# The scaling of a row of summed squares, moved from VectorE into ScalarE's copy of the row

## The chip, the cores and the metric

The kernel runs on one core of a Trainium2 chip. The metric is the device time of one execution in microseconds; the profile is of one execution of the same program.

## What is computed

Three parts follow each other: attention with keys and values pooled by eight (8 batches, 8 heads, 576 positions), a feed-forward block without a nonlinearity, and a second one with a root-mean-square norm ahead of it and a SwiGLU in it. Between the parts the data is a matrix of 4608 tokens by 512 features. The change lies in the norm:

```
a = x @ w1; b = x @ w2; h = a * b @ w3; y = h @ w_out          # first block
rms = sqrt(mean(y * y, axis=-1) + 1e-06); xn = y / rms * rms_g  # norm
g = xn @ w_gate; val = xn @ w_val; out = g * sigmoid(g) * val @ w_out2
```

## The kernel before

Tokens are cut into 9 blocks of 512 (`TB`), held with the features on the partitions: a block of `y` is four tiles of 128 x 512. Every matrix product is done as three products of split operands (`mm3`, lines 104 to 106: high by high, high by low, low by high), so each operand exists as a rounded high part, which ScalarE casts (line 100), and a remainder, which VectorE subtracts (line 101). The two matrices `w3` and `w_out` of the first block are multiplied into one beforehand (`wph`, `wpl`).

The attention and the products with `w1` and `w2` run first, and the products `h` go to DRAM (`hdram`). Then, from about 640 us of the span, the loop of lines 1350 to 1372 takes the nine blocks in the order `OB` (8, 4, 5, 6, 7, 0, 1, 2, 3; `turn` is a block's place in it). For each of eight pieces of a block, `h_load` (line 1311) brings two pieces of `h` into one of three `raw` tiles, `h_split` (lines 100 and 101, tile `hb`) splits them into one of four tiles, and `second` adds 12 matmuls to the block's four PSUM banks. The banks come from two pools of four by the parity of the turn (`ybank`: `ps` or `y`).

After a block, `y_end` squares the four banks on ScalarE (line 679, into `x0b`), copies them out (lines 687 and 689), stores them (line 691, `ydram`) and adds the squares on VectorE (line 693). The rest is a list of steps that the next block's loop takes: `sq_split` splits the sums (ScalarE line 699, VectorE line 701, tile `f`), and four places later `rms` lets TensorE sum them over the partitions with two matmuls by a column of ones into one row of a bank (lines 707 and 708), ScalarE copies the row out of PSUM (line 710), SP stores its 2 KB in DRAM (line 711), POOL loads them back as 128 x 4 (line 713, `ss`), VectorE multiplies by 1/512 and adds 1e-6 (line 714), POOL raises to the power of -0.5 (line 717) and stores the result (line 718, `rdram`). The bank of the row is one of the four that the block after the next block's start needs, so that block's fourth tile waits for the row copy of line 710.

Whoever needs the norm loads `rdram` on all partitions: for block 0, which has turn 5, `xn_steps` does it two turns later (line 1032) and then scales `xr` (line 1042) and splits it (lines 1045 and 1046, `xnh`, `xnl`).

Beside this loop a list of steps (`side`) prepares the weights of the second block: 64-bit inputs are turned into float32 (`Conv`: ScalarE lines 144 and 147, VectorE lines 159, 168 and 171), summed (lines 782 and 933), split (tiles `wst` and `ost`, lines 100 and 101) and stored by POOL (line 798, tensor `wd`; line 943, tensor `od`). The tiles `ost` are used again once their store has landed. SP loads the first weights of the next stage into a ring (`wr`, line 982) as soon as its pieces, used for raw inputs until then, are free.

A scheduler sets the order of the instructions on each engine from these lists and from its own estimates; each engine, and each DMA queue of SP and POOL, then runs in that order.

Of the kernel before, what the change touches and what calls it, by code (L numbers as in the profile page):

```python
# [13 lines left out]
AF = mybir.ActivationFunctionType  # L14
ALU = mybir.AluOpType
# [6 lines left out]
def kernel(  # L22
# [17 lines left out]
    nc = tc.nc  # L40
    B, H, S, D = q.shape
    P = 128
    NT, DM = out.shape
# [25 lines left out]
    def psum():  # L69
        return ps_p.tile([P, 512], F32, tag="ps", name="ps")  # L70
# [8 lines left out]
    def ftile(dt=F32):  # L79
        return f_p.tile([P, 512], dt, tag="f", name="f")  # L80

    def hxtile(nm):
        return hx_p.tile([P, 512], F32R, tag=nm, name=nm)
# [576 lines left out]
    def ybank(i):  # L660
        if turn.get(i, 0) % 2:
            return psum()
        return py_p.tile([P, 512], F32, tag="y", name="y")
# [3 lines left out]
    def bpiece(k):  # L667
        if not x0b:
            for nm in ("xh", "xl"):
                t = x0_p.tile([P, KD, TB], F32R, tag=nm, name="x0b")  # L670
                x0b.extend(t[:, u] for u in range(KD))
        return x0b[k]

    def y_end(i):
        ys = yacc.pop(i)
        sq = []
        for kk in range(KD):
            sq.append(bpiece(kk).bitcast(F32))
            nc.scalar.activation(sq[kk], ys[kk], AF.Square)
            if i == 0:  # L680
                if kk == 0:
                    xr[i, 0] = rtile("xr", F32).rearrange("p (k t) -> p k t", k=KD)
                yc = xr[i, 0][:, kk, :]
            else:
                yc = hxtile("hh" if kk % 2 else "hl").bitcast(F32)
            if kk % 2:
                nc.scalar.copy(yc, ys[kk])
            else:
                nc.vector.tensor_copy(yc, ys[kk])
            if i:  # L690
                nc.sync.dma_start(out=ydram[i, kk], in_=yc)
            if kk:
                nc.vector.tensor_tensor(out=sq[0], in0=sq[0], in1=sq[kk], op=ALU.add)

        sp = []

        def sq_split():
            sp.append(ftile(F32R))
            nc.scalar.copy(sp[0], sq[0])
            sp.append(ftile(F32R))  # L700
            nc.vector.tensor_tensor(
                out=sp[1], in0=sq[0], in1=sp[0].bitcast(F32), op=ALU.subtract
            )

        def rms():
            ps = ybank(i) if turn[i] < NB - 1 else psum()
            nc.tensor.matmul(ps[:1], ones, sp[0], start=True, stop=False)
            nc.tensor.matmul(ps[:1], ones, sp[1], start=False, stop=True)
            row = bpiece(4 + turn[i] % 2).bitcast(F32)
            nc.scalar.copy(row[:1], ps[:1])  # L710
            nc.sync.dma_start(out=sdram[i : i + 1], in_=row[:1])
            ss = const.tile([P, 4], F32, tag="ss", name="ss", bufs=2)
            nc.gpsimd.dma_start(out=ss, in_=sdram[i].rearrange("(p c) -> p c", p=P))
            nc.vector.tensor_scalar(
                out=ss, in0=ss, scalar1=1.0 / DM, scalar2=1e-6, op0=ALU.mult, op1=ALU.add
            )
            nc.gpsimd.tensor_tensor(out=ss, in0=ss, in1=mhalf, op=ALU.pow)
            nc.gpsimd.dma_start(out=rdram[i].rearrange("(p c) -> p c", p=P), in_=ss)

        return [sq_split] + [lambda: None] * 3 + [rms]  # L720
# [18 lines left out]
    def rtile(nm, dt=F32R):  # L739
        return r_ps[0].tile([P, 2048], dt, tag="r", name=nm)  # L740
# [772 lines left out]
```

## Time and profile before

| | us |
|---|---|
| median of 3 runs (lowest, highest) | 1655.96 (1654.37, 1659.35) |
| the profiled execution | 1658.33 |
| its span, first to last instruction | 1656.5 |
| TensorE busy | 1593.1 (96%) |
| VectorE busy | 1099.1 (66%) |
| ScalarE busy | 727.0 (44%) |
| POOL busy | 85.0 (5%) |

A busy time is summed over the whole span. Which engine sets the end in one stretch is read from what each engine waited for there. In a wait, the releaser is the instruction or transfer that ended last before the waiting instruction began; "issue" is time for which the profile shows no releaser.

### The profile page before, as it was taken

What the parts mean: (1) busy time and instruction counts of PE and PEld (TensorE: products, weight loads), DVE (VectorE), ACT (ScalarE), POOL (GpSimd) and SP (SyncE); (2) the same over time, 40 slices, a digit from 0 to 9 for tenths busy, and PEclk for the clock granted to TensorE, in tenths of its full rate; (3) what the DMA queues carried; (4) which work ended last, traced back from release to release, by engine and by line L of the source; (5) the groups of instructions that cost most, each with busy time, mean ns of one, the idle gap of its engine ahead of it and who ended that gap; (6) DMA issues with size and microseconds to landing.
All of it is one profiled execution on the core that took longest, in us unless ns stands there. A gap on an engine that the chain in (4) does not pass through costs nothing.

```text
span 1656.5 us, 22262 instructions
## 1 busy us (share of the span) xinstructions
PE 1593.1 (96%) x8114; PEld 1305.1 (79%) x8114; DVE 1099.1 (66%) x1938; ACT 727.0 (44%) x1700; POOL 85.0 (5%) x107
## 2 busy tenths in 40 slices
PE   6899999999999999998699999999999999999998
PEld 2447778877877788876588888988998898898898
DVE  4676698779787258668636164696477746676456
ACT  4776544444442136555433144244335334344422
POOL 1001101010000000111110000000000000000000
PEclk9999999999999999999899999999999999999999
DMA  9858445554571178686877766668666866676652
GB/s 239 267 168 212 112 113 155 128 150 113 146 247 58 70 267 298 234 295 243 293 259 238 218 214 185 199 190 294 185 194 195 289 191 197 193 239 187 193 182 95
DMA packets 191775, 328.96 MB, mean 199 GB/s; under 512 B 52265, under 2 KB 91177, under 8 KB 186034
## 3 DMA queue, kind: packets, MB, share of 16 engines
q1 hardware_dynamic: 172530, 276.10, 52.8%
q0 software_dynamic: 19136, 51.45, 10.7%
q8 instruction: 64, 1.05, 0.3%
q14 instruction: 45, 0.37, 0.1%
HBM read 250.89 MB, written 76.58 MB: 198 GB/s over the span
## 4 chain that ended last, share of the span: by engine, by line
PE 64%; DMA 5%; DVE 3%; issue 2%; ACT 1%; POOL 0%; SPq 0%; ACTq 0%; POOLq 0%; DVEq 0%
PE ps L104 16%; PE ps L106 16%; PE ps L105 16%; PE y L104 3%; PE y L106 3%; PE y L105 3%; PE o L105 2%; PE o L106 2%; PE o L104 2%; DMA sdram<-x0b 2%; DMA hr<-hd 1%; PE pa L325 1%; PE pa L428 1%; DMA ss<-sdram 1%; DMA od<-ost 1%
## 5 line engine op out<-in xcount | busy, mean ns | idle before, releaser
L104 PE MATMUL ps<-xf,wr 128*128 128x512 f32 x576 | 225.3, 394 | 0.3 <-DVE f L1086 0.2
L105 PE MATMUL ps<-xf,wr 128*128 128x512 f32 x576 | 224.7, 390 | 0.0
L106 PE MATMUL ps<-xf,wr 128*128 128x512 f32 x576 | 224.3, 389 | 0.0
L1086 DVE TENSOR_TENSOR f<-y,f 128x512 f32<-128x512 f32 x48 | 33.1, 689 | 168.2 <-PE y L106 157.0
L368 DVE STREAM_TRANSPOSE aT<-s 32x256 f32<-32x256 f32 x324 | 140.9, 435 | 5.2
L1206 ACT COPY f<-ps 128x512 f32<-128x512 f32 x144 | 84.4, 586 | 128.2 <-PE ps L106 127.1
L104 PEld LDWEIGHTS ps<-xf,wr 128*128 128x128 f32 x576 | 108.1, 188 | 27.4 <-DVE f L1086 5.6
L106 PEld LDWEIGHTS ps<-xf,wr 128*128 128x128 f32 x576 | 108.1, 188 | 22.9
L105 PEld LDWEIGHTS ps<-xf,wr 128*128 128x128 f32 x576 | 108.2, 188 | 21.2
L104 PE MATMUL ps<-xh,w1h 128*128 128x512 f32 x288 | 118.9, 413 | 0.0
L340 ACT ACTIVATE s<-pa,mx 128x72 f32<-128x72 f32 (+1 forms) x280 | 85.7, 333 | 73.1 <-DVE mx L337 73.0
L104 PE MATMUL ps<-xh,w2h 128*128 128x512 f32 x288 | 112.8, 392 | 1.9 <-ACT w2h L100 1.9
L105 PE MATMUL ps<-xl,w1h 128*128 128x512 f32 x288 | 114.2, 397 | 0.0
L106 PE MATMUL ps<-xh,w1l 128*128 128x512 f32 x288 | 113.3, 393 | 0.0
L106 PE MATMUL ps<-xh,w2l 128*128 128x512 f32 x288 | 112.4, 390 | 0.0
L105 PE MATMUL ps<-xl,w2h 128*128 128x512 f32 x288 | 112.2, 389 | 0.0
L634 PE MATMUL wps<-wo,hl 128*128 128x512 f32 x128 | 68.4, 662 | 14.8 <-ACT hl L560 9.1
L572 ACT COPY f<-ps 128x512 f32<-128x512 f32 x72 | 42.9, 600 | 81.7 <-PE ps L106 77.9
L104 PE MATMUL y<-hb,wp 128*128 128x512 f32 x160 | 63.1, 395 | 13.1 <-ACT x0b L710 13.1
L1086 DVE TENSOR_TENSOR f<-ps,f 128x512 f32<-128x512 f32 x96 | 65.0, 687 | 15.4 <-ACT hh L1216 8.2
L1086 DVE TENSOR_TENSOR acc<-ps,acc 128x512 f32<-128x512 f32 x72 | 48.5, 686 | 33.8 <-PE ps L106 19.1
L104 PEld LDWEIGHTS ps<-xh,w1h 128*128 128x128 f32 x288 | 54.8, 190 | 16.6 <-issue 4.7
(245 smaller groups left out, 3945.9 us busy)
## 6 DMA issues: line engine op xcount, KB each, us to landing
wr<-wd SPq DMA_DIRECT2D x168, 512.0 KB
o<-od SPq DMA_DIRECT2D x96, 512.0 KB
wd<-wst POOLq DMA_DIRECT2D x24, 1024.0 KB, 7.1
hr<-hd SPq DMA_DIRECT2D x32, 512.0 KB
od<-ost POOLq DMA_DIRECT2D x12, 1024.0 KB, 8.3
wr<-wd SPq DMA_DIRECT2D x48, 256.0 KB
x1raw<-in_moe_w_dram SPq DMA_DIRECT2D x20, 512.0 KB
hd<-hh SPq DMA_DIRECT2D x36, 256.0 KB
```

What stands on the lines that cost most here:

```text
L104: nc.tensor.matmul(o, lh, rh, start=first, stop=False, skip_group_check=part)
L105: nc.tensor.matmul(o, lh, rl, start=False, stop=False, skip_group_check=part)
L106: nc.tensor.matmul(o, ll, rh, start=False, stop=last, skip_group_check=part)
L325: nc.tensor.matmul(ps[:n, (p % 2) * 2 * SP : (p % 2 + 1) * 2 * SP], qT_t[t // 2][:, t % 2, p, :n], kT[:, p, :], start=True, stop=True,)
L340: nc.scalar.activation(s_t[t][:n, h, :SP], pv[:, j, :], AF.Exp, bias=mx[:, j, :], accum_out=den_t[t][:n, h, :],)
L368: nc.vector.transpose(aT[32 * kb : 32 * kb + 32, :, s0 + 32 * i : s0 + 32 * i + 32], s_t[t][32 * i : 32 * i + 32, :, 32 * kb : 32 * kb + 32],)
L428: nc.tensor.matmul(ps[j * D : (j + 1) * D, :n], st8["vp", b][:, h * D : (h + 1) * D], st8["aT", b][:SP, h, c0 : c0 + n], start=True, stop= ...
L572: nc.scalar.copy(a0[i, m], ps)
L634: nc.tensor.matmul(wps[i], wt[:, i * P : (i + 1) * P], wo[j // 4][:, j % 4, :], start=j == 0, stop=j == KF1 - 1,)
L1086: nc.vector.tensor_tensor(out=out, in0=in0, in1=in1, op=op)
L1206: nc.scalar.copy(t, bank)
```

## The change

ScalarE's copy of the row becomes an activation of the kind Copy, with a scale of 1/512 and a bias of 1e-6, and the VectorE instruction on `ss` is gone:

```diff
@@ -707,13 +707,10 @@
             row = bpiece(4 + turn[i] % 2).bitcast(F32)
-            nc.scalar.copy(row[:1], ps[:1])
+            nc.scalar.activation(row[:1], ps[:1], AF.Copy, scale=1.0 / DM, bias=1e-6)
             nc.sync.dma_start(out=sdram[i : i + 1], in_=row[:1])
             ss = const.tile([P, 4], F32, tag="ss", name="ss", bufs=2)
             nc.gpsimd.dma_start(out=ss, in_=sdram[i].rearrange("(p c) -> p c", p=P))
-            nc.vector.tensor_scalar(
-                out=ss, in0=ss, scalar1=1.0 / DM, scalar2=1e-6, op0=ALU.mult, op1=ALU.add
-            )
             nc.gpsimd.tensor_tensor(out=ss, in0=ss, in1=mhalf, op=ALU.pow)
```

The lines below move up by three. The scheduler, too, gives some instructions another place. On VectorE, after the block of turn 3, the squares are summed (`x0b`) and the next piece split (`hb`); the last line 714 of these rows is that of the row before:

```order
 L693 TENSOR_TENSOR x0b<-x0b 128x512
-L782 TENSOR_TENSOR wf<-wf 128x2x128
+L779 TENSOR_TENSOR wf<-wf 128x2x128
 L689 COPY hl<-ps 128x512
-L714 TENSOR_SCALAR ss<-ss 128x4
 L693 TENSOR_TENSOR x0b<-x0b 128x512 x2
 L101 TENSOR_TENSOR hb<-hr,hb 128x1024
```

Lines 782 and 779 are one instruction under its old and its new number. The last sums and the split no longer stand behind line 714. On ScalarE, ahead of the row copy of turn 5 (the row of block 0), there stood before:

```order
L100 CAST hb<-hr 128x1024
L100 CAST ost<-ot 128x2x256 x4
L144 ACTIVATE raws<-raws 128x512
L100 CAST hb<-hr 128x1024
L710 COPY x0b<-ps 1x512
L144 ACTIVATE raws<-raws 128x512
L147 ACTIVATE f<-raws 128x512
```

and now:

```order
L100 CAST ost<-ot 128x2x256 x4
L100 CAST hb<-hr 128x1024
L144 ACTIVATE raws<-raws 128x512
L147 ACTIVATE f<-raws 128x512
L100 CAST hb<-hr 128x1024
L710 ACTIVATE x0b<-ps 1x512
L144 ACTIVATE raws<-raws 128x512
L100 CAST ost<-of 128x2x256
```

One split of `hb` and one conversion have moved behind the four casts of `ost`. In SP's queue, around the store of that row (line 711), there stood before:

```order
L982 DMA wr<-wd_0_1033 128x2x512
L711 DMA sdram<-x0b 1x512
L1311 DMA hr<-hd_98 128x2x512
L982 DMA wr<-wd_0_1033 128x2x512
L691 DMA ydram<-hl 128x512
```

and now:

```order
L1308 DMA hr<-hd_98 128x2x512
L979 DMA wr<-wd_0_1033 128x2x512 x2
L711 DMA sdram<-x0b 1x512
L1308 DMA hr<-hd_98 128x2x512
L979 DMA wr<-wd_1_1028 128x2x512
```

Both loads of that ring piece now stand ahead of the row's store.

## Rows read from the trace of the kernel before

**Rows 1.** TensorE's waits by line and releaser, 640 to 900 us: total, times, longest
```profile
PE y L104 <- ACT x0b L710: 13.1, 2, 11.0
PE ps L104 <- ACT x0b L710: 6.0, 1, 6.0
PE ps L708 <- DVE f L701: 1.8, 1, 1.8
PE ps L707 <- ACT f L699: 1.0, 1, 1.0
```

**Rows 2.** The same from 840 us to the end
```profile
PE ps L104 <- DVE f L1086: 0.2, 1, 0.2
```

**Rows 3.** 720 to 870 us: length, busy PE, PEld, DVE, ACT, POOL, clock, DMA share, GB/s
```profile
720.00:870.00 150.00, 127.67 (x541) 102.21 (x540) 91.04 (x142) 71.82 (x117) 21.82 (x31) 0.94 0.77 268
```

**Rows 4.** Line 714: what its engine's idle time before it ended with (us, times)
```profile
  DMA ss<-sdram: 24.9, 4
  issue: 16.9, 3
```

**Rows 5.** VectorE in order of time: start, us, instruction, idle time before and releaser
```profile
724.67 0.17 DVE L714 TENSOR_SCALAR ss<-ss 128x4 f32<-128x4 f32 x1 [8.07 <-issue]
...
726.15 1.22 DVE L101 TENSOR_TENSOR hb<-hr,hb 128x1024 fp32r<-128x1024 f32 x1
...
744.86 0.17 DVE L714 TENSOR_SCALAR ss<-ss 128x4 f32<-128x4 f32 x1 [4.72 <-issue]
```

**Rows 6.** ScalarE in order of time
```profile
726.26 0.62 ACT L699 CAST f<-x0b 128x512 fp32r<-128x512 f32 x1 [9.17 <-DVE x0b L693]
...
733.97 0.57 ACT L710 COPY x0b<-ps 1x512 f32<-1x512 f32 x1
...
755.97 1.14 ACT L100 CAST ost<-ot 128x512 fp32r<-128x512 f32 x2
...
760.85 0.57 ACT L710 COPY x0b<-y 1x512 f32<-1x512 f32 x1
...
785.87 2.18 ACT L100 CAST ost<-ot 128x512 fp32r<-128x512 f32 x4 [6.88 <-DMA od<-ost]
787.95 0.67 ACT L144 ACTIVATE raws<-raws 128x512 int32<-128x512 uint32 x1
789.20 1.05 ACT L100 CAST hb<-hr 128x1024 fp32r<-128x1024 f32 x1 [0.58 <-DMA hr<-hd]
790.15 0.57 ACT L710 COPY x0b<-ps 1x512 f32<-1x512 f32 x1
```

**Rows 7.** POOL in order of time: stores of ost
```profile
750.70 0.55 POOL L943 DMA_DIRECT2D od<-ost  x1 [3.29 <-ACT ost L100]
...
776.51 0.55 POOL L943 DMA_DIRECT2D od<-ost  x1 [2.69 <-ACT ost L100]
```

**Rows 8.** The chain that ended last, 750 to 800 us: start, us, what
```profile
751.37 8.45 DMA hr<-hd
...
776.51 9.26 DMA od<-ost
...
790.59 0.52 SPq L982
...
791.20 5.90 DMA sdram<-x0b
```

**Rows 9.** TensorE in order of time: the last two restarts
```profile
790.77 0.80 PE L104 MATMUL ps<-hb,wp 128*128 128x512 f32 x1 [6.01 <-ACT x0b L710]
...
826.54 0.80 PE L104 MATMUL y<-hb,wp 128*128 128x512 f32 x1 [11.04 <-ACT x0b L710]
```

**Rows 10.** Forms of line 710 and of line 435's full tiles: ns min/median/max
```profile
L710 ACT COPY x0b<-ps x5: 566/570/577, 682.5 to 884.3; 1x512 f32<-1x512 f32 x5
...
L435 ACT ACTIVATE xh<-ps x4: 577/586/590, 97.2 to 106.9; 128x512 fp32r<-128x512 f32 x4
```

**Rows 11.** Line 713's loads of ss
```profile
DMA to landing us min/median/max: 1.8/4.8/6.1
```

## The prediction

> **What bounds the kernel now.** The page says TensorE, and almost everywhere it is. What can still be won is where it waits, so I read its waits first, in the stretch in which the changed line runs (640 to 900 us), then from there to the end. In the first it waits 21.9 us in four entries: 13.1 and 6.0 us for ScalarE's row copy of line 710, 1.8 and 1.0 us for the split of the summed squares [rows 1]. In the second it waits 0.2 us [rows 2]. So whatever time it is earlier at the end of the last of those waits, it is earlier at the end of the kernel, and nothing before that wait counts by itself. Call the row copies row 0 to row 8 after the blocks they close. The last wait ends at 826.54, when row 6 has left its bank; the one before ends at 790.77 with row 5 [rows 9]. The stretch from 720 to 870 has TensorE busy for 127.67 of 150 us and moves 268 GB/s [rows 3].
>
> Why do row copies come late? ScalarE runs in order, and what stands ahead of the copy waits for VectorE or a transfer. VectorE in turn stands still at line 714, for the 2 KB that go to DRAM and back: 24.9 us in four waits that the profile names, 16.9 in three that it calls issue [rows 4], 41.8 us together. The ones that matter last 8.07 us (to 724.67) and 4.72 us (to 744.86) [rows 5]; behind each are queued the remaining sums of squares and the next splits of `hb`, for which TensorE and the next `hr` loads wait.
>
> **The change, part by part.** *VectorE:* nine instructions of 0.17 us go [rows 5], 1.5 us of work on an engine with idle time: nothing by itself. With them go the nine waits, and that is the change. *ScalarE:* the copy becomes an activation with a scale and a bias. The nearest row for it is the scaled copy of line 435, also out of PSUM and 512 wide: 586 ns, against 570 ns for the row copy [rows 10]. Nine times 0.016 is 0.14 us, of which at most two lie on the path: nothing. The Trainium skill, "ScalarE: Activation LUTs", section "What ACT_TABLE_LOAD costs", gives 186 ns plus 0.833 ns per element for immediate scale and bias; by it the row would take an estimated 0.61 us, and the sum would be the same within 0.1 us. *POOL:* the power now waits for the loaded squares itself. It waited for them before as well, by way of VectorE, so no wait is added, and what is queued behind it (the stores of `wst` and `ost`) is not held longer. The hop through VectorE goes, its 0.17 us [rows 5] and a signal: 0.2 us a row. *The order:* ScalarE and SP get some rows in another place, shown above; POOL and TensorE keep theirs.
>
> So the sum follows the rows to the last wait.
>
> *Row 3 to row 4.* Row 3 is copied at 733.97, at the end of a run of ScalarE work that starts at 726.26 with the split waiting for VectorE's sums [rows 6]. Without the 8.07 us these sums start at 716.6 (724.67 less 8.07), and the run at 718.2; but a split of `hb` ahead of the copy needs a load issued behind VectorE's split, which ends at 727.4, now at 719.3 [rows 5]; with the longest load shown, 8.45 us [rows 8], and 0.95 us of cast it is some 728.5. In the trace POOL is free for the first `od` store 13.4 us after row 3 (750.70 less 3.29 of waiting for the cast, against 733.97) [rows 6, 7]; less 0.2 this is 741.7, and the casts are then long done. That store must land before two casts of `ost`: with the same 5.3 us at most (issued at 750.70, it was there when ScalarE needed it at 755.97 [rows 6, 7]) 747.0. Two casts (1.1), two of `hb` (0.95 each, 789.20 to 790.15) and two conversions (0.6 each) then stand ahead of row 4 [rows 6]: 751.2, say 751.5 against 760.85 [rows 6]. **9.4 us earlier.** The bounds: only VectorE's own 4.72 us if nothing upstream helps; 12.8 us if both waits, 8.07 and 4.72, come through in full and nothing else is late.
>
> *Row 4 to row 5.* These stand 29.3 us apart [rows 6]: 13.0 until POOL is through with row 4's trip (776.51 less 2.69), 2.69 more for the cast of the second `od` group [rows 7], 9.26 for its store to land [rows 8], and 4.3 of ScalarE's work from 785.87 to row 5 at 790.15, which waited for that landing [rows 6]. The trip loses 0.2. The 2.69 goes, since half of that cast now stands among the squares, before POOL is free. The new order sets a second `hb` cast and a conversion between the landing and the row instead of before it: four casts 2.1 (785.87 to 787.95), then 0.95, 1.2 and 0.95, or 5.2 in place of 4.3. Sum 13.0 - 0.2 + 9.26 + 5.2 = 27.3: **2.0 us less**, row 5 at 778.8. The bounds are 5 less (an emptier store) and 3 more (a fuller one). TensorE first wanted the bank at 784.76 (790.77 less 6.01 [rows 9]); earlier by the waits already gone, 2.8 us for the split and 2.1 for row 4 (13.1 less the longest, 11.0 [rows 1]), that is 779.9: the wait of 6.0 us before row 5 just goes.
>
> *Row 5 to the restart.* 36.4 us in the trace (790.15 to 826.54): the row goes out, comes back, is raised to the power, goes out, comes back on all partitions, scales `xr`, and then ScalarE gets to row 6 [rows 6, 9]. The hop was 0.2 of this. Against it SP now issues two ring loads ahead of row 5's store where it issued one at 790.59, and the first still waits for VectorE to be done with the piece (line 171); the store went out at 791.20, 1.05 us after the row [rows 8]. By the new order VectorE is through with line 171 some 0.8 us after the row, by my estimate (four splits of `ost`, one of `hb` and four conversion steps behind ScalarE's casts), so the store leaves some 1.75 us after the row, 0.7 later than before; and 512 KB more lie ahead of it in the queues, at the stretch's 268 GB/s [rows 3] 2.0 us at most, of which I take half. Sum: 36.4 - 0.2 + 0.7 + 1.0 = 37.9: **1.5 us more.** The bounds: 8.45 more (a whole load as long as the longest) and 4.3 less (below).
>
> Restart at 826.54 - 9.4 - 2.0 + 1.5 = 816.6, **9.9 us earlier**; the wait before it stays about as long as it was, now because the row's trip is longer than TensorE's block. From there all of TensorE's work follows without waits [rows 2]. Against the profiled execution's 1658.33 us that is 1648.4. That execution is 2.4 us above the median of the three runs, 1655.96, and within their spread, so a median may come out at 1646; I keep to the sum and say **1648**.
>
> **The rivals.** *The transfers get quicker too.* The load of `ss` takes 1.8 to 6.1 us, 4.8 in the middle [rows 11]; with VectorE no longer piling up its splits the loads spread, and the row's trips could near the lower end: 3.0 us each for rows 3 and 4, 4.3 for row 5, 10.3 in all, 1648.4 - 10.3 = **1638**. For it: row 5's trip was near the top of the span. Against: the same bytes move in less time. The Trainium skill, "DMA: Bandwidth & Descriptors", section "Anatomy of one DMA — SWDGE (gpsimd) path", gives about 2.0 us fixed for a transfer, by which this case would hold; only the quickest row here agrees with it.
>
> *VectorE was not what held the rows.* POOL keeps the trip and the `od` stores in one queue. If row 4 gains only the 4.72 us, the next step loses nothing and the last costs 2.5 us more (both loads ahead in full), the restart moves 2.2 us: **1656**, no change. For it: the 6.0 us wait is named for a store, not for VectorE. Against: that store was issued late because its cast was.
>
> *Slower.* The store of row 5 sits behind two ring loads on SP. If its 2 KB wait for both as for the longest load shown, 2 x 8.45 us [rows 8], its trip is 16.9 us longer; less the 11.4 us of the first two steps the restart comes 5.5 us later than now: **1664**. It decides from 11.4 us of added trip on. Against: in the trace one such load stood just ahead, and the store landed in 5.90 us [rows 8].
>
> **How the numbers follow.** Forecast 0.62, quicker transfers 0.18, no change 0.14, slower 0.06. About 0.3%, 5 us, is what a measurement of this kernel can tell from none: faster by more 0.80, the same 0.14, slower 0.06. The range goes from 1634, the median of 1655.96 less all 21.9 us of waits, to 1654: the forecast with row 4 earlier by 4.72 only is 1653.1, and some of the no-change case lies below 1654.
>
> **What would show it.** Right: VectorE's wait ahead of the sums is gone, and TensorE's waits for the split and before rows 4 and 5 with it; one wait of 9 to 14 us for row 6 is left, ending at 812 to 820; POOL's power waits for the load of `ss`. Wrong: a restart after 822, a wait before row 5 of over 3 us, or row 5's store over 4 us behind its row; and, on the other side, a wait before row 6 under 6 us.

## The result and the profile after

The changed kernel took 1640.17 us in the median beside 1655.94 for the kernel before on the same chip; the ratio is 0.9893, 95% interval 0.9852 to 0.9934. One of its four executions, 1751.6 us, ran at a granted clock of 0.851 in place of 0.988 to 0.993; it raises this median, while the ratio is of the other three, whose median is 1636.09. The profiled execution took 1635.69 us, its span 1633.8, against 1658.33 and 1656.5. The prediction said 1648, faster.

TensorE is busy for 1587.1 us of the span (1593.1 before); no other engine became the bound. From the page, busy time by engine:

```profile
PE 1587.1 (97%) x8114; PEld 1303.1 (80%) x8114; DVE 1098.5 (67%) x1929; ACT 728.0 (45%) x1700; POOL 86.7 (5%) x107
```

TensorE's waits from 640 to 900 us (line waited at, releaser, total, times, longest), of which four entries with 21.9 us stood in [rows 1] (the same view has a fifth, 0.4 us for a split of `hb`, that is not among them):

```profile
PE y L104 <- ACT x0b L710: 5.1, 1, 5.1
```

The busy time from 720 to 870 us [rows 3], where TensorE had 127.67 us and the core moved 268 GB/s:

```profile
720.00:870.00 150.00, 144.93 (x628) 117.96 (x627) 91.57 (x138) 70.14 (x114) 23.24 (x30) 0.98 0.80 276
```

What the power now waits for, in the view of line 714 (POOL's power, the number it has now; compare [rows 4]), and how long the loads of `ss` take in the view of line 713 [rows 11]:

```profile
  DMA ss<-sdram: 29.5, 9
```

```profile
DMA to landing us min/median/max: 1.8/3.9/5.5
```

VectorE's 41.8 us of waits for the 2 KB are gone; the wait is POOL's, in whose queue it always stood as well. The row copies in ScalarE's order of time, rows 0, 3, 4, 5 and 6 of [rows 6], now:

```profile
657.31 0.58 ACT L710 ACTIVATE x0b<-y 1x512 f32<-1x512 f32 x1
...
724.13 0.58 ACT L710 ACTIVATE x0b<-ps 1x512 f32<-1x512 f32 x1
749.37 0.58 ACT L710 ACTIVATE x0b<-y 1x512 f32<-1x512 f32 x1
771.29 0.58 ACT L710 ACTIVATE x0b<-ps 1x512 f32<-1x512 f32 x1
802.29 0.58 ACT L710 ACTIVATE x0b<-y 1x512 f32<-1x512 f32 x1
```

TensorE's one restart [rows 9]:

```profile
802.93 0.80 PE L104 MATMUL y<-hb,wp 128*128 128x512 f32 x1 [5.08 <-ACT x0b L710]
```

Row 0 itself moved: it is copied at 660.18 before and at 657.31 after. The change cannot do that, since row 0 is the first to run through the changed lines; over the fourteen profiled executions of this study row 0 stands anywhere from 651.4 to 663.0 us. So in what follows every row is counted from row 0 of its own trace:

| row copies, us after row 0 | 1 | 2 | 3 | 4 | 5 | 6 |
|---|---|---|---|---|---|---|
| before | 22.30 | 49.15 | 73.79 | 100.67 | 129.97 | 165.74 |
| after | 22.30 | 44.56 | 66.82 | 92.06 | 113.98 | 144.98 |

Row 6, which releases the last restart, is 20.8 us earlier; 2.9 us lie ahead of row 0, and 0.9 us were lost behind row 6 (the span ends 831.5 us after it, before 830.6). That is the 22.7 us between the spans. In the new trace rows 0 to 3 follow each other at 22.3 us, the time TensorE needs for a block: nothing holds them. In the old one row 2 was already 4.6 us late.

### The profile page after: what moved, and what is told of

Its sections match the earlier page's. It is cut to its first block, busy times and chain, and to the rows that moved or that the text cites. A ratio compares the mean times of both kernels' runs of the same rounds, so it can differ in the third digit from the quotient of the medians.

```text
span 1633.8 us, 22237 instructions
## 1 busy us (share of the span) xinstructions
PE 1587.1 (97%) x8114; PEld 1303.1 (80%) x8114; DVE 1098.5 (67%) x1929; ACT 728.0 (45%) x1700; POOL 86.7 (5%) x107
## 3 DMA queue, kind: packets, MB, share of 16 engines
q8 instruction: 64, 1.05, 0.3%
## 4 chain that ended last, share of the span: by engine, by line
PE 71%; DMA 1%; DVE 1%; issue 1%; ACT 0%; POOL 0%; ACTq 0%; POOLq 0%; SPq 0%
PE ps L104 17%; PE ps L105 17%; PE ps L106 17%; PE y L104 4%; PE y L105 4%; PE y L106 4%; PE o L105 2%; PE o L106 2%; PE o L104 2%; PE pa L325 1%; PE pa L428 1%; DMA f<-rdram 0%; DMA od<-ost 0%; DMA sdram<-x0b 0%; PE pa L307 0%
## 5 line engine op out<-in xcount | busy, mean ns | idle before, releaser
L106 PE MATMUL ps<-o,hf 128*128 128x256 f32 x240 | 67.9, 283 | 0.0
```

The lines of the kernel that those rows point to most:

```text
L106: nc.tensor.matmul(o, ll, rh, start=False, stop=last, skip_group_check=part)
```

## The experiments

The first three ask whether VectorE's wait is the cause, the fourth what the wait for row 6 is made of.

**The changed kernel again**, with no edit.

> The changed kernel itself again. If its shorter steps (22 us from row 4 to row 5, 32 us from row 5 to the restart) belong to the program, they come back within 1 us and the time is 1636 us. If they were the luck of one execution, the steps lie between these and the forecast 27 and 38 us, and the time between 1638 and 1648 us.

Measured: 1636.1 us (1635.02 to 1638.14), ratio 0.9893, interval 0.9874 to 0.9912; rows 4, 5 and 6 at 92.07, 114.08 and 145.19 us after row 0. What the trace shows belongs to the program. These narrower runs are what the following ones are compared with.

**The scale on POOL.** The copy is a copy again, and POOL scales `ss`:

```diff
-            nc.scalar.activation(row[:1], ps[:1], AF.Copy, scale=1.0 / DM, bias=1e-6)
+            nc.scalar.copy(row[:1], ps[:1])
...
+            nc.gpsimd.tensor_scalar(
+                out=ss, in0=ss, scalar1=1.0 / DM, scalar2=1e-6, op0=ALU.mult, op1=ALU.add
+            )
```

> The scaling stands on POOL between the load and the power; ScalarE copies plainly. Theory (the wait that held VectorE was all of it): VectorE's order is that of the changed kernel, TensorE waits only for row 6, and each row's trip is longer by one small POOL operation of 1 to 1.5 us, two trips in line: 1637 to 1641 us. Rival (the gain came from the fewer hops of the trip or from ScalarE's form): the hop is back, so 1650 to 1656 us.

Measured: 1641.72 us, 1 us above the range I gave; ratio 0.9924 (0.9898 to 0.9949). Most of the gain is there, so what matters is that VectorE is out of the trip, not that ScalarE does the scaling. Rows 0 to 4 stand as in the changed kernel (row 4 at 92.01); then row 5 is 7 us later. POOL in order of time shows why: the power of row 4 took nine times its usual 1.03 us, and the store of `ost` behind it left 16.3 us after the row (8.0 in the changed kernel), so that ScalarE's casts waited 9.92 us for it.

```profile
756.23 9.24 POOL L717 TENSOR_TENSOR ss<-ss,mhalf 128x4 f32<-128x4 f32 x1
```

More on this at the end.

**The wait without the work.** The changed kernel, with a VectorE copy of `ss` into a tile that nobody reads, in the place of the old instruction:

```diff
-            nc.gpsimd.tensor_tensor(out=ss, in0=ss, in1=mhalf, op=ALU.pow)
-            nc.gpsimd.dma_start(out=rdram[i].rearrange("(p c) -> p c", p=P), in_=ss)
+            dd = const.tile([P, 4], F32, tag="dd", name="dd", bufs=2)
+            nc.vector.tensor_copy(dd, ss)
+            sr = const.tile([P, 4], F32, tag="sr", name="sr", bufs=2)
+            nc.gpsimd.tensor_tensor(out=sr, in0=ss, in1=mhalf, op=ALU.pow)
+            nc.gpsimd.dma_start(out=rdram[i].rearrange("(p c) -> p c", p=P), in_=sr)
```

> The changed kernel, with a copy of the 128x4 loaded squares into a tile that nobody reads put on VectorE: the wait is back, the trip of the row is as short as in the changed kernel (the power writes a tile of its own, so it does not wait for VectorE). Theory: TensorE's waits for the split (2 to 3 us), before rows 4 and 5 come back, and the time is 1650 to 1657 us. Rival (the shorter trip): 1636 to 1641 us.

Measured: 1659.36 us, 2 us above the range I gave; ratio 1.0038 (1.0024 to 1.0053): by the time the whole gain is gone, though POOL and the rows' trips wait for nothing that VectorE does. TensorE's waits of [rows 1] are back, somewhat shorter:

```profile
PE y L104 <- ACT x0b L710: 8.2, 1, 8.2
PE ps L104 <- ACT x0b L710: 4.5, 1, 4.5
PE ps L708 <- DVE f L701: 1.8, 1, 1.8
PE ps L707 <- ACT f L699: 1.2, 1, 1.2
PE y L105 <- DVE hb L101: 0.4, 1, 0.4
```

Row 6 comes 161.26 us after row 0: 16.3 of the 20.8 us are lost again. The rest of the time is lost behind row 6, not by a wait: the span ends 837.9 us after it, 831.5 in the changed kernel, without a further wait of TensorE. The 1728 matmuls of `xf` by `wr` into `ps` there are busy for 679.6 us in all, 674.3 in the changed kernel, and why stays open. So VectorE's wait makes most of the loss of this run, not all of it. VectorE, in order, held all that was queued behind its copy of `ss`.

**The load of the inverse root one block later.** The wait that is left, for row 6, ends when ScalarE has worked through casts of `ost` (waiting for a store) and two splits `xnh` (waiting for the load of `rdram`). This moves the latter:

```diff
-            if w == turn[0] + 2 and xs:
+            if w == turn[0] + 3 and xs:
```

> The changed kernel with the norm of block 0 asked for one block later. What stands ahead of row 6 on ScalarE behind the load of the row's result falls from nine operations to three. Theory (the wait of 5.1 us before the restart is this in-order wait and nothing else): the wait goes, with the 15 matmuls at half clock behind it some 3 us more, 1627 to 1632 us. Rival (the next stage then waits for the later norm): the wait moves to the first matmul of the next stage and the time is 1634 to 1640 us.

Measured: 1633.94 us (1628.98 to 1638.31), not clear of the changed kernel's 1635.02 to 1638.14, and the wait for row 6 still 4.5 us: it neither went nor moved to the next stage, so neither theory held. The scheduler kept two of the splits ahead of row 6, and POOL's power of row 5 took 4.46 us this time, with the `ost` stores behind it:

```profile
787.70 4.46 POOL L714 TENSOR_TENSOR ss<-ss,mhalf 128x4 f32<-128x4 f32 x1 [4.98 <-DMA ss<-sdram]
792.45 0.59 POOL L715 DMA_DIRECT2D rdram<-ss  x1 [0.29 <-POOL ss L714]
793.05 1.07 POOL L940 DMA_DIRECT2D od<-ost  x2
```

```profile
797.57 2.18 ACT L100 CAST ost<-ot 128x512 fp32r<-128x512 f32 x4 [9.88 <-DMA od<-ost]
...
803.05 1.33 ACT L1042 ACTIVATE xnh<-xr,g_col 128x512 fp32r<-128x512 f32 x2 [2.34 <-DVE xr L1039]
```

So two things hold row 6, the store and the splits, and this run could not tell them apart.

The next question is which of the nine waits counts. These runs scale some rows on VectorE and the others on ScalarE, by one test on the turn:

```diff
-            nc.scalar.activation(row[:1], ps[:1], AF.Copy, scale=1.0 / DM, bias=1e-6)
+            on_dve = turn[i] == 4
+            if on_dve:
+                nc.scalar.copy(row[:1], ps[:1])
+            else:
+                nc.scalar.activation(row[:1], ps[:1], AF.Copy, scale=1.0 / DM, bias=1e-6)
...
+            if on_dve:
+                nc.vector.tensor_scalar(
+                    out=ss, in0=ss, scalar1=1.0 / DM, scalar2=1e-6, op0=ALU.mult, op1=ALU.add
+                )
```

**VectorE for row 4 alone.**

> VectorE scales again for row 4 alone; all other rows by ScalarE as in the change. Theory (the change gains because VectorE no longer stands in front of queued squares and splits while a row's sum goes out and back; row 4's wait is what set the step from row 4 to row 5): rows 3 and 4 as in the changed kernel (725 and 750), step 4 to 5 back from 22.0 to 26 to 29 us, a wait of 2 to 6 us before row 5 again, time 1639 to 1644. Rival (that step is shorter because stores and loads land sooner once rows 2 and 3 are spread out, whatever VectorE does at row 4): step 4 to 5 stays at 22 to 23 us, no wait before row 5, time 1635 to 1638.

Measured: 1637.17 us, ratio 0.9892 (0.9854 to 0.993), step 4 to 5 22.05 us. My theory of this step fell: row 4's wait cost nothing. VectorE's timeline says why, the 2 KB were nearly there when VectorE came to them:

```profile
757.40 0.17 DVE L719 TENSOR_SCALAR ss<-ss 128x4 f32<-128x4 f32 x1 [0.38 <-issue]
```

Before the change the same instruction waited 4.12 us. How long VectorE waits depends on how long the trip takes, and that was 10.7 us from row 4's copy to its power before, 6.0 us after, 6.3 here.

**ScalarE for rows 2, 3 and 4**, VectorE for the other six (`on_dve = turn[i] not in (2, 3, 4)`).

> The change for rows 2, 3 and 4 alone; the other six rows are scaled by VectorE as before. Theory (only the waits that end up ahead of the last two restarts count): nearly all of the gain stays, 1636 to 1641, the only long wait of TensorE again before row 6 with a restart at 802 to 809. Rival (each of the nine waits gives its share, 17 to 20 us over nine rows): six ninths of the gain are lost, 1647 to 1650.

Measured: 1648.32 us (10 runs), ratio 0.9949 (0.9928 to 0.997). My theory fell again, and by its number the rival was right. But the rows do not show equal shares: row 2 comes at 49.12 us and row 4 at 100.07 us, as late as before the change, although no row from 2 to 4 has a VectorE wait. (Row 3, between them, has nearly caught up: 68.19 us. The run with rows 0 and 1 below shows what holds row 4 again.) So I looked for the delay at rows 0 and 1. Reading these two from POOL's timeline of the kernel before the change (stores of `wst`, then the load of row 1's sums)

```profile
681.31 1.09 POOL L798 DMA_DIRECT2D wd<-wst  x2 [9.68 <-DVE wst L101]
691.03 0.56 POOL L713 DMA_DIRECT2D ss<-sdram  x1 [8.63 <-DMA sdram<-x0b]
```

and after it

```profile
675.32 1.09 POOL L795 DMA_DIRECT2D wd<-wst  x2 [6.36 <-DVE wst L101]
684.94 0.56 POOL L713 DMA_DIRECT2D ss<-sdram  x1 [8.53 <-DMA sdram<-x0b]
688.87 1.25 POOL L714 TENSOR_TENSOR ss<-ss,mhalf 128x4 f32<-128x4 f32 x1 [3.38 <-DMA ss<-sdram]
```

beside VectorE's waits before the change

```profile
669.08 0.17 DVE L714 TENSOR_SCALAR ss<-ss 128x4 f32<-128x4 f32 x1 [2.98 <-DMA ss<-sdram]
696.91 0.17 DVE L714 TENSOR_SCALAR ss<-ss 128x4 f32<-128x4 f32 x1 [8.55 <-DMA ss<-sdram]
```

gives a new theory. After row 0 VectorE waits only 2.98 us, and TensorE has slack for it: row 1 is on time, 22.30 us after row 0, in both. But the splits of `wst` are queued behind that wait, and their two stores of 1 MB go out 21.13 us after row 0 in place of 18.01. The load of row 1's sums follows these stores by 9.7 us in the one trace and by 9.6 in the other, although row 1's own store had been issued at nearly the same place (22.98 and 22.91 us after row 0). So it comes 3.2 us later after row 1, and it takes 5.9 us in place of 3.9. The trip is 14.7 us in place of 9.3 from the row's copy to its power, and VectorE, waiting for it, loses 8.55 us: now row 2 is 4.6 us late, the next stores of `wst` leave 47.40 us after row 0 in place of 38.65, row 2's trip takes 15.6 us in place of 9.7, and so on. A wait that is hidden makes the next one three times as long. The last four runs test this.

**VectorE for row 0 alone** (`on_dve = turn[i] == 0`): the first delay, while VectorE does not wait for the longer trip that it makes.

> VectorE scales again for row 0 alone. New theory (a wait of VectorE makes its splits late; the wst stores that follow them then leave 2 us ahead of the next row's 2 KB store in place of 5, so that row's trip takes 14.6 us in place of 9; it costs TensorE time only if VectorE waits for that longer trip too): VectorE waits 3 us after row 0 as before, the wst stores leave 2 to 3 us ahead of row 1's store, row 1's trip from its copy to the power is 13 to 15 us, but VectorE does not wait for it, so rows 4 and 5 stay near 92 and 114 us after row 0 and the time at 1636 to 1640. Rival (the first delay is enough, it runs through POOL's queue alone): rows 4 and 6 near 100 and 155 us after row 0, as in the run with six VectorE rows, time 1645 to 1650.

Measured: 1634.6 us, 1 us under the range I gave; ratio 0.9881 (0.9855 to 0.9906). The `wst` stores left 1.85 us ahead of row 1's store, and row 1's trip took 14.7 us:

```profile
675.14 1.09 POOL L803 DMA_DIRECT2D wd<-wst  x2 [9.69 <-DVE wst L101]
684.82 0.56 POOL L717 DMA_DIRECT2D ss<-sdram  x1 [8.59 <-DMA sdram<-x0b]
691.01 2.04 POOL L722 TENSOR_TENSOR ss<-ss,mhalf 128x4 f32<-128x4 f32 x1 [5.64 <-DMA ss<-sdram]
```

Yet rows 4 and 5 came at 91.98 and 114.40 us. Row 1's long trip is there and costs nothing here, where VectorE does not wait for it.

**VectorE for rows 0 and 1** (`turn[i] < 2`).

> VectorE scales for rows 0 and 1, ScalarE for the other seven. New theory (the two early waits, 3 and 8.5 us, start the chain and the later rows only carry it on): row 2 comes 49 us after row 0 in place of 44.6, row 4 near 100 in place of 92, time 1643 to 1649, as in the run in which VectorE scaled rows 0, 1 and 5 to 8. Rival (what that run lost came from rows 5 and 6, the last before TensorE's last restart): row 4 may be late, but the restart before row 6 is as in the changed kernel, 146 us after row 0, time 1636 to 1639.

Measured: 1641.95 us, ratio 0.9911 (0.9888 to 0.9935); the time is 1 us under the range I gave. Rows 2, 4 and 6 at 49.62, 99.88 and 153.28 us: two instructions of 0.17 us at the start of the stage, with none behind, lose 8.3 of the 20.8 us at row 6. The late TensorE waits are row 4's and row 6's:

```profile
PE y L104 <- ACT x0b L714: 10.4, 2, 5.9
```

The delay is not carried by VectorE alone. Row 3 had nearly caught up (68.71 us, 66.82 in the changed kernel), and VectorE waits for no row after row 1 here, yet row 4 is 7.8 us late. POOL and ScalarE in order of time:

```profile
728.28 1.07 POOL L803 DMA_DIRECT2D wd<-wst  x2
...
743.54 3.48 POOL L722 TENSOR_TENSOR ss<-ss,mhalf 128x4 f32<-128x4 f32 x1 [4.56 <-DMA ss<-sdram]
...
747.91 1.59 POOL L948 DMA_DIRECT2D od<-ost  x3
...
753.64 1.14 ACT L100 CAST ost<-ot 128x512 fp32r<-128x512 f32 x2 [9.81 <-DMA od<-ost]
```

The `wst` stores left 0.97 us ahead of row 3's copy (10.1 us in the changed kernel), the row's trip took 14.3 us (6.9), the `ost` stores behind it left 18.7 us after the row (11.0), and ScalarE's casts waited 9.81 us for them (3.77). Here a long trip cost time through POOL's queue, with VectorE out of it. VectorE for row 1 alone was not run.

**ScalarE for rows 0 and 1 alone** (`turn[i] >= 2`).

> ScalarE scales for rows 0 and 1 alone, VectorE for the other seven as before the change. New theory (with rows 0 and 1 on time the trips of rows 2 to 4 are 9, 7 and 6 us, and VectorE waits for them little): VectorE's waits after rows 2 to 4 are under 4 us each in place of 8.1, 4.7 and 4.1, rows 4 and 5 within 4 us of the changed kernel's 92 and 114 us after row 0, time 1636 to 1643. Rival (every row's wait counts as much as another): two ninths of the gain, time 1648 to 1654, the waits after rows 2 to 4 as before the change.

Measured: 1640.71 us, ratio 0.9903 (0.9885 to 0.9921). With rows 0 and 1 on time, VectorE's waits after rows 2, 3 and 4 shrink from 8.07, 4.72 and 4.12 us to

```profile
705.10 0.17 DVE L719 TENSOR_SCALAR ss<-ss 128x4 f32<-128x4 f32 x1 [3.17 <-issue]
724.68 0.17 DVE L719 TENSOR_SCALAR ss<-ss 128x4 f32<-128x4 f32 x1 [0.28 <-issue]
750.17 0.17 DVE L719 TENSOR_SCALAR ss<-ss 128x4 f32<-128x4 f32 x1 [3.20 <-issue]
781.72 0.17 DVE L719 TENSOR_SCALAR ss<-ss 128x4 f32<-128x4 f32 x1 [6.33 <-DMA ss<-sdram]
```

and rows 4, 5 and 6 come at 89.05, 116.95 and 151.74 us. Two of nine rows bring 14.0 of the 20.8 us at row 6. Of the 6.8 us that are missing 3.0 are there at row 5, and 3.8 come in the step behind it, where VectorE still waits 6.33 us. The shares of the rows do not add up (14.0 by rows 0 and 1 alone, 12.5 by the other seven alone), since they cut the same delay. They are read from one trace each; by the times, these two runs cannot be told from the changed kernel, whose interval was 0.9874 to 0.9912.

**The `ost` stores moved to SP.** POOL's queue holds a row's trip and, behind it, stores that ScalarE's casts wait for. In the changed kernel:

```diff
-            nc.gpsimd.dma_start(
+            nc.sync.dma_start(
                 out=odram[g][:, 2 * z : 2 * z + 2], in_=cells[g].pop(z).bitcast(F32)
             )
```

> The changed kernel with the stores of the ost groups issued by SP in place of POOL, so that they no longer stand behind a row's trip in POOL's queue. Theory (the trip holds the next row by way of the store behind the power in POOL's queue): step 4 to 5 falls below 20 us and the wait for row 6 to 0 to 4 us, time 1629 to 1635. Rival (SP's queue turns into the hold: stores that wait for ScalarE's casts stand ahead of loads of hr and of the row's own store): hr loads come late, new waits of TensorE, time 1640 or more.

Measured: 1628.81 us (1623.42 to 1633.97), ratio 0.9836 (0.9791 to 0.9882). TensorE has no wait left between 640 and 900 us; row 6 comes 136.56 us after row 0, 8.4 us ahead of the changed kernel's. The step from row 4 to 5 is 21.76 us, not under 20: I had left out that TensorE's own block sets the pace at 22.3 us; rows that are on time cannot come faster.

The same edit in the kernel before the change:

> The kernel before the change with the ost stores issued by SP in place of POOL; VectorE scales all nine rows. If the early waits and their wst stores, which stay on POOL, make the chain, rows 2 to 4 are as late as before (49, 74 and about 100 us after row 0), only the steps behind row 4 get shorter, and the time falls to 1643 to 1650, above the 1629 of the changed kernel with the same edit. Rival (the ost stores in POOL's queue are all that holds the rows, and the scale is worth nothing without them): 1626 to 1634.

Measured: 1638.7 us, ratio 0.9897 (0.9882 to 0.9911), better than I expected and not as good as the rival. Rows 2 to 4 are as late as before (49.22, 73.90, 98.01), which is the chain from row 0; behind row 4 the rows catch up (121.84, 148.93), which is the store. TensorE's waits lie ahead of 800 us now, and none is for a row copy:

```profile
PE ps L105 <- DVE hb L101: 3.3, 1, 3.3
PE ps L708 <- DVE f L701: 1.8, 1, 1.8
PE ps L707 <- ACT f L699: 1.1, 1, 1.1
```

So there are two holds, each worth much the same alone; with the stores moved, the scale is still worth 12.4 us at row 6 (148.93 less 136.56).

**The splits behind row 6.** The last hold, in the changed kernel:

```diff
-            if w == turn[0] + 2 and xs:
+            if xs and w == turn[0] + 3 and m >= 8:
```

> The changed kernel with the load of the inverse root and the four scaled splits of block 0 moved behind row 6 on ScalarE. Theory (what holds row 6 in the changed kernel is, first, the store of the second ost group behind the power on POOL and, second, the four splits that wait for the inverse root): with the second gone the wait for row 6 falls from 5 us to 0 to 1 if the power of row 5 takes its 1 us, and to 3 to 4 if it is stretched to 4.5 as in the run with the loads one block later; time 1629 to 1633. Rival (the splits are not what holds row 6, or what is gained there is lost when the block 0 product needs them): wait and time as in the changed kernel, 1635 to 1638, or a new wait after 830.

Measured: 1629.7 us (1625.82 to 1630.89), ratio 0.9844 (0.9801 to 0.9888). The power of row 5 took 4.52 us, and the wait for row 6 was 2.7 us with row 6 at 142.57. The splits did hold row 6: with a power of nearly the same length (4.46 us) two of them ahead of row 6 left a wait of 4.5 us. This version and the one with SP's stores beat both kernels: no run of either took as long as the 1635.0 of the changed kernel's fastest in its repeat. That repeat ran on another chip, and the intervals of the ratios still overlap a little, so how much they gain over the changed kernel is not settled. The two edits together were not run.

## Why the prediction was right, and where its sum was off

The direction held, and the time lies in the range, in its lower part: 1648 was 8 us above the measured median and 12 us above that of the repeat. The restart came 23.6 us earlier, where the sum said 9.9; 2.9 of them lie ahead of row 0, of which no term could know.

*What bounds the kernel.* Right: TensorE's waits, and VectorE's stand behind the 2 KB as their cause. The wait without the work brings 16.3 of the 20.8 us at row 6 back.

*VectorE, ScalarE, POOL by themselves.* Right: the row copy went from 570 to 582 ns, 0.012 us where I took 0.016, and the work saved on VectorE shows nowhere. The Trainium skill, "ScalarE: Activation LUTs", section "What ACT_TABLE_LOAD costs", came to an estimated 0.61 us; the row says 0.58.

*Row 3 to row 4.* Right in size, in part by luck: row 4 is 8.6 us earlier after row 0, where I said 9.4, because misses cancelled. Row 3 came 7.0 us earlier, not 5.5, and POOL was free 11.0 us after it, not 13.2; but the `ost` casts began 7.5 us after their store was issued, not 5.3, and ScalarE needed 6.8 us from there to row 4, not 4.5, for 2.59 us of which it waited for VectorE's line 171. The sum had nothing for that wait. Its cause, too, was read too late in the chain. I took the waits of 8.07 and 4.72 us [rows 5] as the ones that matter; the runs show that they were long because VectorE had waited 2.98 and 8.55 us after rows 0 and 1. With those two gone, the same instructions waited 3.17 and 0.28 us.

*Row 4 to row 5.* This term was mis-sized: 27.3 us forecast, 21.9 measured, 29.3 before. I left the trip at 12.8 us and the store's landing at 9.26 us. They were 7.96 (row 4 at 749.37, the store at 757.33) and 6.02 us; ScalarE's part behind the landing was 7.8 us, not 5.2, with the same wait (2.58 us) in it. From the chain of waits after:

```profile
757.33 6.02 DMA od<-ost
...
772.01 5.34 DMA sdram<-x0b
...
784.77 1.74 DMA rdram<-ss
786.57 6.80 DMA f<-rdram
```

*Row 5 to the restart.* Mis-sized too, and with the wrong sign: 37.9 us forecast, 31.6 measured, 36.4 before. I added 0.7 us for SP's order and 1.0 for a ring load ahead of the row's store. The store left 0.72 us after row 5 (1.05 before) and landed in 5.34 us (5.90 before [rows 8]); from the row to the power it was 12.2 us (13.9 before), and the store of the inverse root took 1.74 us (4.17 before).

Both misses are one: I kept each transfer at its old length, and 12.1 of the 20.8 us lie in trips and landings that became shorter (4.6 for row 4's copy to its power, 3.2 for the store behind it, 1.8 for row 5's copy to its power, 2.4 for the store of the inverse root). That is the first rival, *the transfers get quicker too*, to which I gave 0.18 and 1638 us; the median of 1636.1 us in the repeated runs is nearest to it. Its reason was sound (VectorE no longer piles up its splits, so the stores spread), and my argument against it, that the same bytes move in less time, was not: when the bytes of `wst` move decides how long the 2 KB take, as row 1's trip shows (14.7 us with VectorE for row 0 alone, 9.3 without). For the stores of `ost` that was not tried. The sentence cited there from the Trainium skill, "DMA: Bandwidth & Descriptors", section "Anatomy of one DMA — SWDGE (gpsimd) path", about 2.0 us fixed, fits the quickest load of `ss` (1.8 us, before and after) and says nothing of the median, which went from 4.8 to 3.9 us.

*VectorE was not what held the rows* fell; a part of it was true, since the `ost` stores behind the trip are a hold of their own. *Slower* fell: nothing piled up ahead of row 5's store.

*What would show it.* TensorE's waits for the split and before rows 4 and 5 are gone, as forecast. The wait before row 6 is 5.1 us and the restart at 802.9, where I had 9 to 14 us and 812 to 820; "under 6 us" stood there as the sign that I was wrong on the other side, and it was. What stays open is how the two 1 MB stores delay the row's 2 KB: the load of the sums followed them by 9.6 to 9.7 us in the traces shown, whether by the queues that both go through or by POOL's issue, and no run parts these.

## What to carry to other kernels

A tiny instruction that waits for a DRAM round trip on an in-order engine costs what is queued behind it, and its wait grows if that work feeds transfers which stand in the way of the next round trip; put the wait on an engine with little behind it (POOL was not free of such work either: its stores were the second hold). Look for the first such wait in the chain, even one that is hidden: here freeing the first two of nine rows brought 14.0 of 20.8 us, although freeing only the other seven brought 12.5. And when delays are priced, do not keep the transfers at their old length, since they shift with the work.

## What the runs showed of the hardware

*POOL's power beside VectorE.* The instruction works on 128 x 4 elements. Wherever VectorE was idle beside it, it took 1.03 us. Beside a VectorE without a gap it took 1.0 to 1.5 us in most cases, but 3.12 us after row 3 in the changed kernel, 4.46 and 9.24 us in the two runs above, and in the one with SP's stores

```profile
760.20 15.06 POOL L714 TENSOR_TENSOR ss<-ss,mhalf 128x4 f32<-128x4 f32 x1 [4.79 <-DMA ss<-sdram]
```

while VectorE ran mostly subtractions and sums of two operands from SBUF without a gap, the first of them here:

```profile
760.50 1.22 DVE L101 TENSOR_TENSOR hb<-hr,hb 128x1024 fp32r<-128x1024 f32 x1
761.64 0.68 DVE L101 TENSOR_TENSOR ost<-of,ost 128x512 fp32r<-128x512 f32 x1
762.24 0.68 DVE L701 TENSOR_TENSOR f<-x0b,f 128x512 fp32r<-128x512 f32 x1
```

The powers of 4.46, 4.52 and 9.24 us each ended 0.90 us after such a run of VectorE's had ended, which is about the time that a power takes beside an idle VectorE. In the old kernel the power, which started just behind VectorE's instruction, took 1.40 to 1.44 us in six of nine rows. The Trainium skill, "SBUF — State Buffer", section "SBUF: two separate sides", says that of a VectorE instruction with two SBUF inputs and a GpSimd instruction that reads SBUF the one that starts first has the port pair that they share for its whole length, and the other is blocked. The rows agree that the power can be held, but for many VectorE instructions (none shown is longer than 1.22 us), not for one; that it is that port was not tried, and spans on POOL are rough. That it was no fault of the record alone is shown by the stores: in the run with 4.46 us they left only when the power had ended.

*The time ahead of the stage* varies by more than the effect of many edits: row 0 stood at 651.4 to 663.0 us in programs that are alike up to there. Two profiles are therefore best compared from a common point, not by their spans.

*The clock behind a wait.* After TensorE's wait of 5.08 us the granted clock is 0.50 for a while, the 1.2 GHz level of 2.4; ahead of the wait and later it is 1.00. Three stretches of the changed kernel (columns as in [rows 3]):

```profile
790.00:797.80 7.80, 7.80 (x35) 6.15 (x33) 4.41 (x8) 2.28 (x3) 0.54 (x1) 1.00 0.88 311
803.00:807.50 4.50, 4.50 (x11) 3.53 (x12) 4.50 (x7) 4.30 (x8) 1.22 (x3) 0.50 0.84 346
808.50:820.00 11.50, 11.50 (x52) 9.29 (x51) 3.16 (x5) 0.62 (x1) 2.69 (x2) 1.00 0.72 211
```

Half a clock for 4.5 us is 2.25 us of lost work, so this wait cost nearly half as much again as it lasted. What a wait costs in this way differs: in the 10 us from the copy of row 6 on, TensorE did 35 matmuls at a mean granted clock of 0.83 before the change (after a wait of 11.04 us), 31 at 0.72 after it, and 41 at 1.00 in the run with the splits behind row 6 (after a wait of 2.7 us). The four matmuls between the first two, at some 0.22 us each (52 in 11.5 us above), are the 0.9 us lost behind row 6.
